# Three expert loads set between the turning transfers of block 10, a pack load ahead of half of block 9's, and the slot sums of block 10 one expert step later

## The chip, the cores and the metric

The kernel runs on one core of a Trainium2 chip. The metric is the device time of one execution in microseconds (us). The kernel before takes 660.15 us, the median of three runs (659.58 to 660.9).

## The reference, cut to what matters

Three layers follow each other on 4608 tokens of width 512, all in float32:

```python
scores = scale * q @ k.T                     # 64 pairs (batch, head), 576 positions, head width 64
x = ((scores * decay) @ v)                   # causal decay gamma_h ** (i - j), then tokens x 512
h = x @ w_in; g = h * sigmoid(1.702 * h)     # 512 -> 2048
x = g @ w_out                                # 2048 -> 512
logits = x @ phi                             # 32 slots
d = softmax over tokens(logits); slot_input = d.T @ x
slot_out[e] = relu(slot_input[e] @ w1[e]) @ w2[e]      # 8 experts, 4 slots each, 512 -> 1024 -> 512
out = softmax over slots(logits) @ slot_out
```

The logits and the softmax over tokens need every token before any expert can start. So the experts' weights (w1 and w2, 64 pieces of 512 KB) and w_out (8 pieces) are used only after the last token.

## The kernel before

The tokens go through in 12 blocks of 384 (`n` = 0 to 11; block 10 is the second last, 11 the last). A block has 16 expert steps `fc`, one for each 128 of the 2048 hidden columns. In each, TensorE (PE) makes 12 products into `hp` (L349), ScalarE (ACT) puts the gated result into `gT` (L359), and VectorE (DVE) turns it into `pre` (L378). Beside this run the steps of the attention of the next block: three steps of 128 tokens to a block, `step_of(g)`, each of which ends by loading the `pack` (q, k and v, 1 MB) of step g + 2 on SyncE's queue (SP, L179). There are two pack buffers; the load of step 35, the last, waits for the products of step 33.

What one half block has in `pre` (8 hidden steps) goes to `nat` in 16 transfers of 96 KB from on-chip memory to on-chip memory, four for each of four row groups `a` (`shuffle`, L386): rows of 1 KB, 32 partitions to 32 others. When both halves lie in `nat`, the slot sums of that block are made one block later: `slots_part(n - 1)`, 12 matmuls into `Sg` (L453, two profile rows to a matmul in float32), and DVE adds them to `acc` (L459). `nat` is one buffer for all blocks. In block 11 the turning is done by PE itself (`turn_fc`, `tpg`, L373) and ACT or DVE copies each result to `nat` (L374), so these copies come after the slot sums of block 10. `Sg`, `tpg` and the attention's results share the same three PSUM buffers.

All order is written out by hand, engine by engine. All transfers and loads stand in one queue, that of SP, and are issued in the order of the code. `prefetch` takes the next piece of a fixed list (8 of w_out, 32 of w1, 32 of w2, three of w1 first) and loads it to the next place that has come free: the buffers of x of block 10 (three pieces), of `pre` (three), of the weights `w` of each expert step of block 11, of `gT`, and so on (L501). After the slot sums of block 11 (`Sg`, L605, in `tail`) come five new places, the reused ones, the expert layers (`h_ps` L666, `so_ps` L707), and the results `op` (L728) with the output transfers (L737).

Of the kernel before, what the change touches and what calls it, by code (L numbers as in the profile page):

```python
# [9 lines left out]
F32 = mybir.dt.float32  # L10
# [22 lines left out]
LAST = NBLK - 1  # L33
NFC = DFF // 128
NDC = DM // 128
NTILE = NT // 128
GF = 4
# [32 lines left out]
EARLY_WINDOWS, EARLY_LOGITS, EARLY_EXP_AT, EARLY_TURN_AT = (2, 6, 10), (((1, 3),), ((0, 0),), ((0, 1),)), 3, 5  # L70
LATE_TURNS = {**{fc: () for fc in range(4)}, 4: (0, 1), 5: (2, 3), 6: (4, 5), 7: (6, 7)}
LAST_LOGITS = {0: ((1, 2), (1, 3)), 4: ((0, 0),), 8: ((0, 1),), 12: ((0, 2),)}
LAST_TURNS = {6: (0, 1), 7: (2, 3), 8: (4, 5), 9: (6, 7), 10: (8,), 11: (9,)}
LAST_EXP_AT, LAST_TURN_AT, LAST_SLOTS_AT = 1, 3, 6
LAST_ACT = (0, 2, 4, 6, 8, 11, 12, 13, 15)
NPRE = NTILE - 2 * NT128

# [52 lines left out]
def tile_kernel(ctx, tc, qkv, w_in, w_turned, w_out, phi, w1, w2, consts, out):  # L130
# [11 lines left out]
    pb = ctx.enter_context(tc.tile_pool(name="pb", bufs=1, side="right", reuse_waits="tile"))  # L142
# [50 lines left out]
    def products(g, parts=("out", "state", "score")):  # L193

        n, cb = g + 1, g % NPB
        own, out_ = [], []
        if "out" in parts and g >= 0:
            t = packs[g]
            Op = Ops[g] = ps.tile([128, NP, NSEQ, C], F32, tag="r", name="Op", bufs=3)
            for p, j in pairs:  # L200
                if cb:
                    out_.append((Op, t, SS, QT, p, j, True))
                out_.append((Op, t, VN, SC, p, j, cb == 0))
        if "state" in parts and g >= 0 and cb < NPB - 1:
            if cb == 0:
                St[g // NPB] = ps.tile([128, NP, NSEQ, D], F32, tag="St", name="St")
            own += [(St[g // NPB], packs[g], KN, VN, p, j, cb + p + j == 0) for p, j in pairs]
        if "score" in parts and n < NSTEP:
            Sp = Sps[n] = ps.tile([128, NP, NSEQ, C], F32, tag="r", name="Sp", bufs=3)
            own += [(Sp, packs[n], KT, QT, p, j, True) for p, j in pairs]  # L210
        for i in range(max(len(own), len(out_))):
            for what, turn in ((own, 0), (out_, 1)):
                if i < len(what):
                    o, w, a, b, p, j, first_ = what[i]
                    for h, oh in ((lo, (lo, hi)[turn]), (hi, (hi, lo)[turn])):
                        pe.matmul(o[oh, p, j, :], w[h, a, p, j], w[h, b, p, j], start=first_, stop=True,  # L216
                                  skip_group_check=True)
# [6 lines left out]
    def scale_scores(n):  # L224
        if n < NSTEP:
            dve.tensor_tensor(packs[n][:, SC], Sps.pop(n), across(dtab), op=ALU.mult)  # L226
# [22 lines left out]
    def step_of(g, between):  # L249
        products(g)  # L250
        scale_keys(g + 1)
        scale_scores(g + 1)
        scale_state(g + 1)
        between()
        scale_out(g)
        x_high(g)
        x_low(g)
        if g + 2 < NSTEP:
            load_step(g + 2)
# [121 lines left out]
    def shuffle(n, hf, rows=range(4)):  # L381
        if n not in nat:
            nat[n] = pm.tile([128, NT128, 4, NFC, 32], F32, tag="nat", name="nat")
        for a in rows:
            for b in range(4):
                sp.dma_start(nat[n][32 * b:32 * b + 32, :, a, hf * HF:(hf + 1) * HF, :],  # L386
                             pre[n, hf][32 * a:32 * a + 32, :, b])
# [60 lines left out]
    def slots_part(n):  # L448
        Sg = ps.tile([128, 4, 4, 32], F32, tag="r", name="Sg", bufs=3)
        for c in range(NT128):  # L450
            nv = nat[n][:, c].rearrange("p a f i -> p f a i")
            for b in range(4):
                pe.matmul(Sg[32 * b:32 * b + 32], dn[n][:, c, :], nv[:, 4 * b:4 * b + 4],  # L453
                          start=(c == 0), stop=(c == NT128 - 1))
        sg = Sg.rearrange("p f a i -> p (f a i)")
        if n == 0:
            dve.tensor_copy(acc, sg)
        else:
            dve.scalar_tensor_tensor(acc, acc, st["corr"], sg, op0=ALU.mult, op1=ALU.add)  # L459
# [19 lines left out]
    wx, places = {}, []  # L479
# [4 lines left out]
    def prefetch(place=None):  # L484
        if not todo:
            return
        key = todo.pop(0)
        if place is None:
            place = places.pop(0)
        t = place()  # L490
        if key not in kept:
            places.append(place)
        if key[0] == 0:
            src = wo_dram[key[1]] if wide else wo_dram[key[1] * 256:(key[1] + 1) * 256, :].rearrange(
                "(c p) d -> p c d", p=128)
        elif key[0] == 1:
            src = w1[key[1], key[2] * 128:(key[2] + 1) * 128, :].rearrange("(c p) d -> p c d", p=128)
        else:
            src = w2[key[1], key[2]]
        t = t.rearrange("p (c d) -> p c d", c=src.shape[1])  # L500
        sp.dma_start(t, src)  # L501
        wx[key] = t

    def prefetch_views(t):
        for i in range(t.shape[1]):
            prefetch(lambda i=i: t[:, i])
# [251 lines left out]
    with tc.manual_schedule(engines={getattr(mybir.EngineType, e) for e in ("PE", "Activation", "DVE", "Pool", "SP")}):  # L758
        for x in START:
            step(x)  # L760
        for n in range(2, LAST):
            early = n == LAST - 1
            windows, logits = (EARLY_WINDOWS, EARLY_LOGITS) if early else (WINDOWS, WINDOW_LOGITS)
            for fc in range(NFC):
                main_fc(n, fc)
                for f in LATE_TURNS.get(fc, (fc,)) if n == 2 else (fc,):
                    turn_fc(n, f)
                if fc in KEEP_AT and n < 2 + NFC // 2 and wide:
                    keep_w_out(2 * (n - 2) + KEEP_AT[fc][0], KEEP_AT[fc][1])
                if fc in windows:  # L770
                    i = windows.index(fc)

                    def between():
                        for m, k in logits[i]:
                            logits_group(n - m, k)
                        if i == 0:
                            softmax_split(n - 1)

                    step_of((n + 1) * STEPS + i, between)
                    if i == 1:  # L780
                        slots_part(n - 1)
                if fc == max(windows[1], HF - 1):
                    shuffle(n, 0)
                if fc == (EARLY_EXP_AT if early else EXP_AT):
                    softmax_exp(n - 1)
                if fc == (EARLY_TURN_AT if early else TURN_AT):
                    softmax_turn(n - 1)
                if fc == NFC - 1:
                    shuffle(n, 1)
                if n == 3 and fc == 0:  # L790
                    prefetch_views(ring4[:, 1:4])
                if n == LAST - 1:
                    if fc == 2:
                        prefetch_views(ring4[:, 0:1])
                        prefetch(place_in(px, "raw", 1))
                    if fc == windows[-1]:
                        att_ctx.close()
                        pw2 = ctx.enter_context(tc.tile_pool(name="pw2", bufs=NW2, side="right", reuse_waits="tile"))
                        for _ in range(NW2):
                            prefetch(place_in(pw2, "w", NW2))  # L800
                        prefetch_views(pb.tile([128, 3, 1024], F32, tag="pre", name="wx", bufs=2))
        n = LAST
        for fc in range(NFC):
            main_fc(n, fc)
            if fc in LAST_LOGITS:
                for m, g in LAST_LOGITS[fc]:
                    logits_group(n - m, g)
            if fc == 0:
                softmax_split(n - 1)
                prefetch_views(pb.tile([128, 3, 1024], F32, tag="x", name="wx", bufs=1))  # L810
            if fc == LAST_EXP_AT:
                softmax_exp(n - 1)
                combine_part(0, NPRE)
            if fc == LAST_TURN_AT:
                softmax_turn(n - 1)
            if fc == LAST_SLOTS_AT:
                slots_part(n - 1)
                prefetch_views(pb.tile([128, 3, 1024], F32, tag="pre", name="wx", bufs=2))
            for f in LAST_TURNS.get(fc, ()):
                turn_fc(n, f)  # L820
            if fc < NFC - 1:
                prefetch(place_in(pw, "w", NFC))
            if fc == GF:
                third = gate().rearrange("p l t -> p (l t)")
                prefetch(lambda: third[:, 0:1024])
        tail()
# [43 lines left out]
```

## Time and profile before

| | |
|---|---|
| median of three runs | 660.15 us (659.58 to 660.9) |
| the profiled execution | 662.24 us, of which 660.5 us span |
| PE busy | 635.4 us (96%) |
| DVE, ACT, POOL busy | 45%, 33%, 12% |
| granted TensorE clock | 0.997 over the span |
| DMA queue of SP | 149.43 MB, 71.1% of 16 engines' span |

PE counts as busy while modelled matmuls run, so 96% leaves little, but not nothing: idle times of PE and stretches in which a group of matmuls takes longer than the same group elsewhere both count. The DMA share is an average: in slices of 16.5 us the page shows 143 to 182 GB/s in the middle of the run and 373 to 411 GB/s in the last eight slices but one.

### The profile page before, as it was taken

What the parts mean: (1) busy time and instruction counts of PE and PEld (TensorE: products, weight loads), DVE (VectorE), ACT (ScalarE), POOL (GpSimd) and SP (SyncE); (2) the same over time, 40 slices, a digit from 0 to 9 for tenths busy, and PEclk for the clock granted to TensorE, in tenths of its full rate; (3) what the DMA queues carried; (4) which work ended last, traced back from release to release, by engine and by line L of the source; (5) the groups of instructions that cost most, each with busy time, mean ns of one, the idle gap of its engine ahead of it and who ended that gap; (6) DMA issues with size and microseconds to landing.
All of it is one profiled execution on the core that took longest, in us unless ns stands there. A gap on an engine that the chain in (4) does not pass through costs nothing.

```text
span 660.5 us, 19533 instructions
## 1 busy us (share of the span) xinstructions
PE 635.4 (96%) x8601; PEld 545.2 (83%) x8601; DVE 295.3 (45%) x592; ACT 221.1 (33%) x430; POOL 80.4 (12%) x72
## 2 busy tenths in 40 slices
PE   6898999999999999999999999999999999999994
PEld 6797787898988989989989989889899788874663
DVE  3899923354463453443444533634535323122143
ACT  2783532141242242332412412412424124240143
POOL 2103101202111011121111011111211000001000
PEclk9999999999999999999999999999999999999998
DMA  8997648676676747737646657467566498999998
GB/s 322 401 314 272 257 97 224 161 197 161 189 243 175 204 164 192 201 113 200 177 135 184 178 143 208 134 163 198 182 175 143 158 287 236 411 406 373 408 410 329
DMA packets 67732, 150.67 MB, mean 228 GB/s; under 512 B 8768, under 2 KB 42944, under 8 KB 63040
## 3 DMA queue, kind: packets, MB, share of 16 engines
q1 hardware_dynamic: 67648, 149.43, 71.1%
q8 instruction: 67, 1.10, 0.7%
q14 instruction: 17, 0.14, 0.1%
HBM read 101.16 MB, written 13.63 MB: 174 GB/s over the span
## 4 chain that ended last, share of the span: by engine, by line
PE 81%; DMA 7%; SPq 4%; DVE 3%; ACT 2%; issue 1%; POOL 0%; DVEq 0%; ACTq 0%
PE hp L349 51%; PE Lg L393 5%; PE Sg L453 4%; SPq L386 4%; PE Sp L216 4%; PE St L216 3%; PE so_ps L707 2%; DMA early_raw<-in_w_turned_dram 2%; PE Op L216 2%; PE h_ps L666 2%; PE op L728 2%; DMA pack<-in_qkv_dram 2%; DMA early_raw<-in_moe_w_in_dram 1%; PE tpg L373 1%; DMA raw<-in_w_turned_dram 1%
## 5 line engine op out<-in xcount | busy, mean ns | idle before, releaser
L349 PE MATMUL hp<-x,w 128*128 128x384 f32 x2304 | 421.3, 340 | 1.3 <-POOL x L246 1.3
L349 PEld LDWEIGHTS hp<-x,w 128*128 128x128 f32 x2304 | 397.1, 188 | 28.6 <-issue 21.7
L378 DVE STREAM_TRANSPOSE pre<-gT 128x384 f32<-128x384 f32 x172 | 96.3, 571 | 166.4 <-ACT gT L359 158.1
L359 ACT ACTIVATE gT<-hp 128x384 f32<-128x384 f32 x188 | 91.8, 491 | 230.6 <-PE hp L349 230.4
L246 POOL TENSOR_TENSOR x<-xs,x 128x512 fp32r<-128x512 f32 x33 | 42.6, 1292 | 317.0 <-ACT x L241 317.0
L216 PE MATMUL Op<-pack 64*64 64x64 f32 x2176 | 72.5, 221 | 0.2 <-issue 0.2
L216 PEld LDWEIGHTS Op<-pack 64*64 64x64 f32 x2176 | 67.2, 136 | 0.6 <-issue 0.6
L222 POOL TENSOR_TENSOR pack<-pack,cs 128x512 f32<-128x512 f32 x32 | 34.7, 1086 | 137.8 <-DMA pack<-in_qkv_dram 128.6
L241 ACT CAST x<-xs 128x512 fp32r<-128x512 f32 x36 | 22.3, 620 | 83.9 <-DVE xs L234 83.8
L216 PE MATMUL Sp<-pack 64*64 64x64 f32 x1152 | 41.4, 223 | 7.3 <-DMA pack<-in_qkv_dram 7.3
L216 PEld LDWEIGHTS Sp<-pack 64*64 64x64 f32 x1152 | 38.0, 139 | 8.6 <-DMA pack<-in_qkv_dram 7.0
L216 PEld LDWEIGHTS St<-pack 64*64 64x64 f32 x1024 | 33.1, 137 | 7.6 <-issue 7.5
L226 DVE TENSOR_TENSOR pack<-Sp,cs 128x512 f32<-128x512 f32 x36 | 24.8, 688 | 32.1 <-PE Op L216 19.1
L393 PE MATMUL Lg<-gT,Wp 128*32 128x384 f32 x376 | 38.5, 495 | 0.4 <-DVE Lall L440 0.4
L216 PE MATMUL St<-pack 64*64 64x64 f32 x1024 | 37.5, 224 | 0.0
L453 PE MATMUL Sg<-nat,dn 128*32 128x512 f32 x264 | 31.2, 593 | 0.0
L234 DVE TENSOR_TENSOR xs<-Op,cs 128x512 f32<-128x512 f32 x36 | 24.6, 682 | 5.6 <-PE Op L216 5.5
L290 ACT ACTIVATE early_raw<-early_raw 128x512 f32<-128x512 f32 x28 | 19.0, 691 | 14.8 <-DMA early_raw<-in_w_turned_dram 9.7
L230 DVE TENSOR_TENSOR pack<-St,cs 128x512 f32<-128x512 f32 x32 | 21.8, 681 | 4.6 <-PE St L216 3.2
L453 PEld LDWEIGHTS Sg<-nat,dn 128*32 128x32 f32 x264 | 8.8, 110 | 17.5 <-issue 17.4
L290 ACT ACTIVATE raw<-raw 128x512 f32<-128x512 f32 x20 | 13.7, 686 | 19.6 <-DMA raw<-in_moe_w_out_dram 18.4
L459 DVE SCALAR_TENSOR_TENSOR acc<-acc,corr,Sg 128x512 f32<-128x512 f32 x10 | 7.5, 748 | 27.6 <-PE Sg L453 27.6
(131 smaller groups left out, 385.6 us busy)
## 6 DMA issues: line engine op xcount, KB each, us to landing
pack<-in_qkv_dram SPq DMA_DIRECT2D x36, 1024.0 KB, 5.9
nat<-pre SPq DMA_DIRECT2D x352, 96.0 KB, 2.2
wx<-in_moe_w_dram SPq DMA_DIRECT2D x56, 512.0 KB, 9.8
raw<-in_moe_w_out_dram SPq DMA_DIRECT2D x16, 512.0 KB, 4.2
early_raw<-in_moe_w_in_dram SPq DMA_DIRECT2D x15, 512.0 KB, 6.8
out_dram<-wx SPq DMA_DIRECT2D x14, 512.0 KB, 7.6
early_raw<-in_w_turned_dram SPq DMA_DIRECT2D x13, 512.0 KB, 9.3
wo_dram<-ring SPq DMA_DIRECT2D x16, 256.0 KB, 2.0
```

What stands on the lines that cost most here:

```text
L216: pe.matmul(o[oh, p, j, :], w[h, a, p, j], w[h, b, p, j], start=first_, stop=True, skip_group_check=True)
L222: pool.tensor_tensor(k, k, by_state(ksc[:, n % NPB, :]), op=ALU.mult)
L226: dve.tensor_tensor(packs[n][:, SC], Sps.pop(n), across(dtab), op=ALU.mult)
L234: dve.tensor_tensor(xss[g], Ops.pop(g), across(osc), op=ALU.mult)
L246: (eng or pool).tensor_tensor(xl[b_][:, :, cols_], xss.pop(g).rearrange("p a j c -> p a (j c)"), xh[b_][:, :, cols_], op=ALU.subtract)
L290: act.activation(upper, upper, AF.Prelu, scale=2.0 ** -112, alpha=2.0 ** 32)
L349: pe.matmul(hp, wt[fc][:, a, dc, :], b[n][:, dc, :], start=(i == 0), stop=(i == 3 * NDC - 1))
L359: act.activation(gT[n, g][:, fl, :], hps.pop((n, fc)), AF.Gelu_apprx_sigmoid)
L378: dve.transpose(pre[n, hf][:, :, :, fh, :].rearrange("p c b i -> p (c b) i"), gT[n, g][:, fl, :].rearrange("p (x j) -> p x j", j=32))
L386: sp.dma_start(nat[n][32 * b:32 * b + 32, :, a, hf * HF:(hf + 1) * HF, :], pre[n, hf][32 * a:32 * a + 32, :, b])
L393: pe.matmul(Lg[n][32 * fl:32 * fl + 32, :], Wp[:, g * GF + fl, :], gT[n, g][:, fl, :], start=(g == 0), stop=(g == NFC // GF - 1))
L453: pe.matmul(Sg[32 * b:32 * b + 32], dn[n][:, c, :], nv[:, 4 * b:4 * b + 4], start=(c == 0), stop=(c == NT128 - 1))
```

## The change

Four edits. First, in block 9 only two of the four row groups of the second half's transfers are issued at the block's end; the other two follow in block 10 behind its first attention step, and so behind the pack load that this step issues. Second, at the end of block 10 the three loads into the buffer of x stand between the four row groups of that block's transfers, one behind each of the first three; before, they stood behind all of them, in block 11. Third, the slot sums of block 10 are made behind expert step 7 of block 11, not 6, and the turning of hidden steps 0 to 3 of block 11 with them. Fourth, the three loads into the buffer of `pre` are issued at expert step 4 instead of 6.

```diff
--- before.py
+++ after.py
@@ -70,8 +70,8 @@
 EARLY_WINDOWS, EARLY_LOGITS, EARLY_EXP_AT, EARLY_TURN_AT = (2, 6, 10), (((1, 3),), ((0, 0),), ((0, 1),)), 3, 5
 LATE_TURNS = {**{fc: () for fc in range(4)}, 4: (0, 1), 5: (2, 3), 6: (4, 5), 7: (6, 7)}
 LAST_LOGITS = {0: ((1, 2), (1, 3)), 4: ((0, 0),), 8: ((0, 1),), 12: ((0, 2),)}
-LAST_TURNS = {6: (0, 1), 7: (2, 3), 8: (4, 5), 9: (6, 7), 10: (8,), 11: (9,)}
-LAST_EXP_AT, LAST_TURN_AT, LAST_SLOTS_AT = 1, 3, 6
+LAST_TURNS = {7: (0, 1, 2, 3), 8: (4, 5), 9: (6, 7), 10: (8,), 11: (9,)}
+LAST_EXP_AT, LAST_TURN_AT, LAST_SLOTS_AT = 1, 3, 7
 LAST_ACT = (0, 2, 4, 6, 8, 11, 12, 13, 15)
 NPRE = NTILE - 2 * NT128
 
@@ -777,6 +777,8 @@
                             softmax_split(n - 1)
 
                     step_of((n + 1) * STEPS + i, between)
+                    if early and i == 0:
+                        shuffle(n - 1, 1, (2, 3))
                     if i == 1:
                         slots_part(n - 1)
                 if fc == max(windows[1], HF - 1):
@@ -785,8 +787,14 @@
                     softmax_exp(n - 1)
                 if fc == (EARLY_TURN_AT if early else TURN_AT):
                     softmax_turn(n - 1)
-                if fc == NFC - 1:
-                    shuffle(n, 1)
+                if fc == NFC - 1 and not early:
+                    shuffle(n, 1, (0, 1) if n == LAST - 2 else range(4))
+                if fc == NFC - 1 and early:
+                    xv = pb.tile([128, 3, 1024], F32, tag="x", name="wx", bufs=1)
+                    for a in range(4):
+                        shuffle(n, 1, [a])
+                        if a < 3:
+                            prefetch(lambda a=a: xv[:, a])
                 if n == 3 and fc == 0:
                     prefetch_views(ring4[:, 1:4])
                 if n == LAST - 1:
@@ -807,7 +815,6 @@
                     logits_group(n - m, g)
             if fc == 0:
                 softmax_split(n - 1)
-                prefetch_views(pb.tile([128, 3, 1024], F32, tag="x", name="wx", bufs=1))
             if fc == LAST_EXP_AT:
                 softmax_exp(n - 1)
                 combine_part(0, NPRE)
@@ -815,6 +822,7 @@
                 softmax_turn(n - 1)
             if fc == LAST_SLOTS_AT:
                 slots_part(n - 1)
+            if fc == GF:
                 prefetch_views(pb.tile([128, 3, 1024], F32, tag="pre", name="wx", bufs=2))
             for f in LAST_TURNS.get(fc, ()):
                 turn_fc(n, f)
```

On SP's queue, in blocks 9 and 10 (nat<-pre are the transfers, pack the attention's load, ring and wx the first two pieces of w_out):

```order
 L179 DMA pack_93<-in_qkv_dram 128x2048
 L333 DMA wo_dram<-ring 128x512
-L386 DMA nat<-pre 32x3x256 x16
+L386 DMA nat<-pre 32x3x256 x8
 L179 DMA pack_92<-in_qkv_dram 128x2048
+L386 DMA nat<-pre 32x3x256 x8
 L501 DMA ring<-wo_dram 128x1024
 L501 DMA wx<-wo_dram 128x1024
```

The last pack load has moved ahead of eight of the sixteen transfers; nothing else of this piece has moved.

On SP's queue at the end of block 10 and in block 11 (wx and gT are places of expert weights):

```order
 L501 DMA wx<-in_moe_w_dram 128x1024 x5
-L386 DMA nat<-pre 32x3x256 x16
+L386 DMA nat<-pre 32x3x256 x4
+L501 DMA wx<-in_moe_w_dram 128x1024
+L386 DMA nat<-pre 32x3x256 x4
+L501 DMA wx<-in_moe_w_dram 128x1024
+L386 DMA nat<-pre 32x3x256 x4
+L501 DMA wx<-in_moe_w_dram 128x1024
+L386 DMA nat<-pre 32x3x256 x4
 L501 DMA wx<-in_moe_w_dram 128x1024 x8
 L501 DMA gT<-in_moe_w_dram 128x1024
-L501 DMA wx<-in_moe_w_dram 128x1024 x17
```

Three loads have moved ahead of the last twelve, eight and four transfers; the 17 loads behind the first gT become 14.

On PE in block 11, from expert step 5 on (hp are the products of an expert step, 12 matmuls; Sg the slot sums of block 10; tpg the turning, three matmuls to a hidden step):

```order
 L393 MATMUL Lg<-gT,Wp 32x384 x4
-L349 MATMUL hp<-x,w 128x384 x24
+L349 MATMUL hp<-x,w 128x384 x36
 L453 MATMUL Sg<-nat,dn 32x512 x12
-L373 MATMUL tpg<-ident,gT 128x128 x6
-L349 MATMUL hp<-x,w 128x384 x12
-L373 MATMUL tpg<-ident,gT 128x128 x6
+L373 MATMUL tpg<-ident,gT 128x128 x12
 L349 MATMUL hp<-x,w 128x384 x12
```

The products of step 7 now stand ahead of the slot sums, and four turnings follow these in a row.

## Rows read from the trace of the kernel before

**Rows 1.** Timeline of PE, 495 to 600: start, length, line, group [idle before <-releaser].
```profile
502.14 0.23 PE L216 MATMUL Op<-pack 64*64 64x64 f32 x2
...
513.29 0.23 PE L216 MATMUL Op<-pack 64*64 64x64 f32 x2
514.66 0.27 PE L216 MATMUL Sp<-pack 64*64 64x64 f32 x2 [1.14 <-DMA pack<-in_qkv_dram]
...
516.42 2.76 PE L453 MATMUL Sg<-nat,dn 128*32 128x512 f32 x24
...
559.46 3.58 PE L453 MATMUL Sg<-nat,dn 128*32 128x512 f32 x24
```

**Rows 2.** Chain of waits in order of time: start, length, engine, line, count.
```profile
502.48 0.62 SPq L386
503.14 1.67 SPq L386
509.47 5.14 DMA pack<-in_qkv_dram
...
516.60 2.57 PE Sg L453 x24
...
555.17 4.36 PE hp L349 x24
559.53 3.51 PE Sg L453 x24
563.04 0.81 PE tpg L373 x6
563.85 2.09 PE hp L349 x12
565.94 0.66 PE tpg L373 x6
```

**Rows 3.** Timeline of SP's queue, 495 to 600 and 588 to 602: start, length, issues.
```profile
496.44 12.93 SPq L386 DMA_DIRECT2D nat<-pre  x16
...
522.66 10.30 SPq L386 DMA_DIRECT2D nat<-pre  x16
...
542.32 16.25 SPq L386 DMA_DIRECT2D nat<-pre  x16
558.68 1.50 SPq L501 DMA_DIRECT2D wx<-in_moe_w_dram  x3
...
596.17 2.63 SPq L501 DMA_DIRECT2D wx<-in_moe_w_dram  x5
```

**Rows 4.** Line 453, 555 to 565: waits before the slot sums, first and last.
```profile
L453 PEldq EVENT_SEMAPHORE  x8: 51/51/51, 556.3 to 560.2; - x8
```

**Rows 5.** Timeline of SP's queue, 558 to 560: the last transfer's issue.
```profile
557.97 0.60 SPq L386 DMA_DIRECT2D nat<-pre  x1
```

**Rows 6.** The page, section 6: DMA issues, KB each, median us from issue to landing.
```profile
nat<-pre SPq DMA_DIRECT2D x352, 96.0 KB, 2.2
```

**Rows 7.** Stretches: length, busy by engine, clock, DMA share, GB/s.
```profile
545.00:550.00 5.00, 5.00 (x30) 5.00 (x29) 1.81 (x6) 3.26 (x7) 0.00 (x0) 1.00 1.02 398
550.00:555.00 5.00, 4.56 (x32) 3.70 (x30) 3.90 (x8) 3.12 (x5) 0.00 (x0) 1.00 0.82 180
555.00:560.00 5.00, 5.00 (x32) 4.25 (x28) 0.00 (x0) 0.93 (x2) 0.00 (x0) 1.00 0.63 126
565.00:570.00 5.00, 5.00 (x38) 4.09 (x37) 0.56 (x1) 1.38 (x4) 0.00 (x0) 1.00 1.03 415
596.00:597.00 1.00, 0.40 (x6) 0.20 (x2) 0.86 (x2) 0.00 (x0) 0.00 (x0) 1.00 0.47 188
650.00:655.00 5.00, 2.45 (x26) 2.12 (x21) 2.49 (x8) 2.09 (x7) 0.00 (x0) 1.00 1.01 405
```

**Rows 8.** Waits of SP's queue, 542 to 560 and 560 to 597: total us, times, longest.
```profile
SPq L386 <- DMA wx<-in_moe_w_dram: 4.2, 5, 1.5
...
SPq L501 <- PE Sg L605: 3.0, 1, 3.0
```

**Rows 9.** Tile nat, 540 to 565: its transfers' time to landing.
```profile
DMA to landing us min/median/max: 2.2/4.0/7.2
```

**Rows 10.** Timeline of DVE and ACT, 555 to 568: what empties PSUM behind the slot sums.
```profile
563.08 0.75 DVE L459 SCALAR_TENSOR_TENSOR acc<-acc,corr,Sg 128x512 f32<-128x512 f32 x1 [8.91 <-PE Sg L453]
563.88 0.56 DVE L374 COPY nat<-tpg 128x384 f32<-128x384 f32 x1
...
563.56 0.48 ACT L374 COPY nat<-tpg 128x384 f32<-128x384 f32 x1 [3.50 <-PE tpg L373]
```

## The prediction

> **What bounds the kernel now.** I read the timeline of PE first, since PE is busy for nearly the whole span, and looked for places where it stands still or where a group takes longer than the same group elsewhere. Between 500 and 597 us there are two that a transfer causes. At 513.5 the scores of attention step 35 stand still 1.14 us for the last pack load [rows 1]. At 559.46 the slot sums of block 10 begin at once, yet the 24 rows of this group take 3.58 us where the same group took 2.76 at 516.42 [rows 1]; in the chain of waits, which does not count overlap twice, it is 3.51 against 2.57 [rows 2]. The 0.94 us between them is a wait inside the group: the semaphores ahead of these matmuls are waited for until 560.2 [rows 4], and the last of the 16 transfers was issued at 557.97 [rows 5], which with the usual 2.2 us to landing [rows 6] gives 560.2 too. So the group starts on the half of `nat` that is there and waits for the other.
>
> Next I read SP's queue, which issues both kinds. The pack load at 509.47 stands behind 16 transfers that took 12.93 us to issue; the last transfers of block 10 took 16.25 us, and the 16 of the first half before them 10.30 [rows 2, 3]. They took so long because they were issued behind loads: the queue waited five times, 4.2 us in all, for loads to land [rows 8].
>
> Last I read the stretches for the DMA engines. They move 398 GB/s to 550 and 415 GB/s from 565 on, but 180 and 126 GB/s from 550 to 560, at busy shares of 0.82 and 0.63 [rows 7]. Then they are full up to 655, but for one hole: in 596 to 597 they move 188 GB/s [rows 7], because the five loads issued at 596.17 waited 3.0 us for the slot sums of block 11 on PE [rows 3, 8]. That hole decides how much the loads are worth. What lies ahead of it, the DMA engines finish in time; what lies behind it starts when PE gets there. Behind it stand 28 loads and the whole output, and these are full-rate work. So the end follows the time at which PE finishes the slot sums of block 11, and PE between 500 and 596 sets that.
>
> **The change part by part.** The sum is made in the profiled execution's time, 662.24 us (span 660.5), and carried over as a difference to the median of 660.15.
>
> Pack load ahead of eight transfers. It removes the wait of 1.14 us. The eighth transfer was issued at 502.48 and the ninth at 503.14 [rows 2]; the pack load now takes that ninth place, where the products of step 33, which free its buffer, are over (502.37, [rows 1]). The issue at 503.14 was a slow one of 1.67 us [rows 2]; if the pack's is as slow it is out by 504.8, and with the 5.14 us that the load took [rows 2] it lands by 510, 3.5 us ahead of the need at 513.5. Gain: 1.14 us. It adds 0.5 us of issue and 2.5 us of traffic (1 MB at 415 GB/s, [rows 7]) ahead of the other eight transfers. These were all issued by 509.4; now by about 510, landing at 512 to 513. The slot sums of block 9 need them at 516.42 − 1.14 = 515.3 [rows 1]. Cost taken: 0. The far end is 1.2 us: if the last of them, issued at 509.3, takes the longest landing that this kind shows behind loads, 7.2 us [rows 9], it lands at 516.5.
>
> Three loads between the transfers. Before, the last transfer landed at 560.2. Two limits say when it does now. By issue: three more issues of 0.5 us each (1.50 for three, [rows 3]) give 557.97 + 1.5 + 2.2 = 561.7. By traffic: a load takes 1.26 us at 415 GB/s, three 3.8 us; in 550 to 560 the DMA engines were free for 5 × 0.18 + 5 × 0.37 = 2.75 us [rows 7], so 1.05 us is left over, and the last lands at about 561.3. I take 561.7. If the loads fill no gap at all, it is 560.2 + 3.8 = 564.0. If they cost nothing, 560.2.
>
> The Trainium skill has a rule that speaks for the far end: by "DMA: Bandwidth & Descriptors", section "Queues, rings and completion order", each DMA engine takes its descriptors in ring order, so a transfer behind a load has to wait for that load. The trace agrees where loads came first: the transfers of block 10 waited for loads five times. By that alone the last transfer would land at 564.0; the gaps between the transfers are why I don't take it.
>
> Slot sums behind step 7. PE reaches them 2.09 us later in its work [rows 2], and all of this stands 1.14 us earlier, since block 10's chain follows PE from 515 on (the first half's transfers at 522.66, the loads behind them, then the second half's). In the old time scale the waiting matmuls are now due at 559.46 + 2.09 + 0.2 = 561.75, the 0.2 being the first two of the group's rows. Against 561.7 nothing is left of the wait; I take 0.1 us, with 2.25 us (564.0) as the far end and 0 as the near one. Gain: 0.94 − 0.1 = 0.84 us.
>
> Four turnings in a row. Before, two pairs took 0.81 and 0.66 us with the products of step 7 between them [rows 2]. Now the third wants the PSUM buffer of the slot sums, which DVE's addition holds from 563.08 to 563.83 [rows 10], 0.8 us after the sums end at 563.04; PE is then through two turnings in 0.66 to 0.81. The fourth wants the buffer of the first, which ACT copied from 563.56 to 564.04 [rows 10]. With some 0.1 us of signal on each this costs 0.25 us; 0 and 0.6 are the bounds. It was covered by step 7's products before; that cover is gone.
>
> Loads of `pre` at step 4, and the three loads themselves. The number of loads ahead of 596 stays the same and they only start earlier; PE waits for none of them between 560 and 596. Taken at 0. What the DMA engines win there becomes a longer hole ahead of the slot sums of block 11.
>
> Sum: −1.14 − 0.84 + 0.25 = −1.73 us, so 660.51 in the profiled execution and 660.15 − 1.73 = 658.4 as the median. Bounds by term: the pack −1.14 to +0.06, the slot sums −0.94 to +1.31, the turnings 0 to 0.6.
>
> **The rivals.** A: the load costs its issue and its transfer one after the other, three times 0.5 + 1.26 = 5.3 us, so the last transfer lands at 565.5. For it: the 16 issues took 16.25 us in place of 10.30 while loads were in front [rows 3]. Against: 0.37 of the engines' time was free from 555 on. The wait is then 3.75 us: −1.14 − 0.94 + 0.25 + 3.75 = +1.9, so 662.1. It turns the change to a loss from a landing at 563.6, and to one that can be measured from 564.9.
>
> B: the transfers land late by the loads' whole 3.8 us, by ring order alone. The wait is 2.25 us: +0.4, so 660.6; with a third of it hidden, 659.3. This is the case of the Trainium skill's rule above.
>
> C: the pack's wait is not there in an ordinary run. For it: it rests on a few slow issues, 12.93 us for 16 where another 16 took 10.30 [rows 3]; without these 2.6 us the load would have been in time. Against: slow issues are in the stretch of block 10 too. The rest is −0.84 + 0.25 = −0.6: 659.55.
>
> D: the DMA engines bound the whole end from 560 on, so that 3.8 us of loads ahead are 3.8 us off the end: 656.3. For it: 405 to 415 GB/s up to 655 [rows 7]. Against: the hole at 596, which shows that they had nothing to do.
>
> **How the numbers follow.** Forecast 0.50, A 0.08, B 0.17, C 0.17, D 0.08. The forecast's own range is −2.1 to −0.9. A measurement of this kernel can tell 0.2%, 1.3 us, from no change. About three quarters of the forecast (0.38), all of D and a little of B and C (0.04) are faster by that: 0.50. Most of A and a little of the unknown is slower: 0.08. The rest is the same: 0.42. The range that leaves out A's upper half and D's lower goes from 656.8 to 660.7.
>
> **What would show it.** In the profile after: no idle time at the scores of step 35, with the pack load issued near 503; the slot sums of block 10 in 2.6 to 2.8 us behind step 7; some 0.25 us of idle PE at the third turning; more than 126 GB/s in the stretch of the transfers; a longer hole ahead of the slot sums of block 11, and those at about 594.5 instead of 596. If the slot sums still take over 4 us, A or B is right. If those of block 11 end as early as said but the end does not move with them, the reading of the hole is wrong.

## The result, and the profile after

The change makes the kernel slower: 664.68 us (median of five, 662.73 to 665.88) against 659.58. The ratio on record is 1.006, with a 95% interval of 1.0039 to 1.0081; the two medians alone stand 0.8% apart. The forecast was 658.4 us.

The timeline of PE in the changed kernel, with the lines that answer to [rows 1, 2] (start, length, group, idle time before it and who ended it):

```profile
513.68 0.85 PE L393 MATMUL Lg<-gT,Wp 128*32 128x384 f32 x8
514.35 2.76 PE L453 MATMUL Sg<-nat,dn 128*32 128x512 f32 x24
...
553.03 6.51 PE L349 MATMUL hp<-x,w 128*128 128x384 f32 x36
559.47 1.05 PE L453 MATMUL Sg<-nat,dn 128*32 128x512 f32 x4
562.94 2.77 PE L453 MATMUL Sg<-nat,dn 128*32 128x512 f32 x20 [2.41 <-DMA nat<-pre]
565.64 1.78 PE L373 MATMUL tpg<-ident,gT 128*128 128x128 f32 x12
...
594.16 2.78 PE L605 MATMUL Sg<-nat,dn 128*32 128x512 f32 x24 [0.35 <-DVE dn L600]
```

The wait for the pack load is gone: the slot sums of block 9 come straight behind the logits. The slot sums of block 10 begin at 559.47 behind step 7, do their first four rows, and then PE waits until 562.94 for a transfer. In this view the group took 3.58 us before and takes 6.24 now (562.94 + 2.77 − 559.47), where it takes 2.78 without a wait. The wait that the step was to cover has grown from 0.8 us (0.94 in the chain of waits) to 3.46.

SP's queue in the same stretch, with the issue of each part (start, length, count):

```profile
501.79 0.33 SPq L179 DMA_DIRECT2D pack<-in_qkv_dram  x1
502.16 5.93 SPq L386 DMA_DIRECT2D nat<-pre  x8
...
540.49 4.41 SPq L386 DMA_DIRECT2D nat<-pre  x4
545.57 0.33 SPq L501 DMA_DIRECT2D wx<-in_moe_w_dram  x1
546.79 4.90 SPq L386 DMA_DIRECT2D nat<-pre  x4
551.73 0.59 SPq L501 DMA_DIRECT2D wx<-in_moe_w_dram  x1
552.37 3.10 SPq L386 DMA_DIRECT2D nat<-pre  x4
555.51 0.96 SPq L501 DMA_DIRECT2D wx<-in_moe_w_dram  x1
556.51 2.56 SPq L386 DMA_DIRECT2D nat<-pre  x4
559.17 5.65 SPq L501 DMA_DIRECT2D wx<-in_moe_w_dram  x8
```

The 16 transfers and three loads are issued from 540.49 to 559.07, 18.6 us where 16.25 were taken before [rows 3]. The last was issued at 558.4. How long they then took, from the same tile and line as [rows 9, 4]:

```profile
DMA to landing us min/median/max: 4.6/6.7/9.6
...
L453 PEldq EVENT_SEMAPHORE  x8: 51/51/3485, 556.3 to 562.8; - x8
```

No transfer lands in less than 4.6 us; before, the median was 4.0 and the quickest 2.2. That alone makes no wait: in d_swap below, which has none, the quickest took 4.1. The stretches of this profile, against [rows 7]:

```profile
550.00:555.00 5.00, 4.57 (x30) 3.65 (x29) 2.02 (x5) 1.08 (x3) 0.00 (x0) 1.00 1.06 257
555.00:560.00 5.00, 5.00 (x31) 4.37 (x29) 0.00 (x0) 1.40 (x3) 0.00 (x0) 1.00 0.99 252
560.00:565.00 5.00, 2.59 (x22) 0.79 (x20) 0.00 (x0) 0.07 (x1) 0.00 (x0) 1.00 1.04 344
580.00:585.00 5.00, 5.00 (x33) 4.12 (x32) 0.00 (x0) 0.98 (x2) 0.00 (x0) 1.00 0.69 250
585.00:590.00 5.00, 5.00 (x34) 4.00 (x33) 1.04 (x2) 2.36 (x4) 0.00 (x0) 1.00 0.77 244
```

The last two of these before:

```profile
580.00:585.00 5.00, 5.00 (x33) 4.38 (x33) 0.00 (x0) 0.98 (x2) 0.00 (x0) 1.00 1.03 410
585.00:590.00 5.00, 5.00 (x32) 3.62 (x31) 1.12 (x2) 3.22 (x6) 0.00 (x0) 1.00 1.01 392
```

From 550 to 560 the DMA engines are now full and move 2.5 MB in place of 1.5. So the loads did go into the free time, but the transfers paid for it. What was won comes back as free time at 580 to 590, where before the engines were full: SP's queue stands there until PE has freed the places for the next loads.

### The profile page after: what moved, and what is told of

Its sections match the earlier page's. It is cut to its first block, busy times and chain, and to the rows that moved or that the text cites. A ratio compares the mean times of both kernels' runs of the same rounds, so it can differ in the third digit from the quotient of the medians.

```text
span 660.9 us, 19536 instructions
## 1 busy us (share of the span) xinstructions
PE 637.6 (96%) x8601; PEld 547.1 (83%) x8601; DVE 295.0 (45%) x592; ACT 221.7 (34%) x430; POOL 80.3 (12%) x72
## 4 chain that ended last, share of the span: by engine, by line
PE 82%; DMA 7%; DVE 4%; SPq 3%; issue 1%; ACT 1%; POOL 0%; ACTq 0%; DVEq 0%
PE hp L349 52%; PE Lg L393 5%; PE Sg L453 4%; PE St L216 4%; PE Sp L216 4%; DMA wx<-in_moe_w_dram 3%; PE so_ps L707 2%; PE op L728 2%; PE h_ps L666 2%; PE Op L216 2%; DMA pack<-in_qkv_dram 2%; SPq L386 2%; PE tpg L373 1%; SPq L501 1%; DVE pre L378 1%
## 5 line engine op out<-in xcount | busy, mean ns | idle before, releaser
L453 PE MATMUL Sg<-nat,dn 128*32 128x512 f32 x264 | 31.4, 593 | 2.4 <-DMA nat<-pre 2.4
L453 PEld LDWEIGHTS Sg<-nat,dn 128*32 128x32 f32 x264 | 8.7, 110 | 20.2 <-issue 16.8
L736 DVE COPY wx<-op 128x256 f32<-128x256 f32 (+1 forms) x32 | 11.3, 402 | 19.7 <-PE op L728 19.1
```

## The experiments

Kernels whose labels begin with the same letter were measured in turn with the kernel before on one chip; c, d, e and f are four chips, so ratios are compared between them and not times. The table gives the ratio to before, and from the timeline of PE in each profile the stretch from the begin of the slot sums of block 9 to the begin of those of block 11, with the length of the slot sums of block 10 in it (begin of the first row to end of the last; 2.8 us is no wait). Both leave out the wait for the pack load, which lies ahead of the stretch. Between kernels with the slot sums behind step 6 and behind step 7 the stretch differs by the four turnings in a row too.

| kernel | loads ahead of the last transfer, against before | ratio (95%) | stretch, us | slot sums 10, us |
|---|---|---|---|---|
| before, profile above | 0 | | 76.86 | 3.58 |
| c_before | 0 | 1.0001 (0.998 to 1.0021) | 77.96 | 4.66 |
| c_pack | 0 | 1.0003 (0.9984 to 1.0022) | 77.20 | 3.91 |
| c_behind | 0 | 0.9984 (0.9966 to 1.0002) | 76.36 | 2.78 |
| d_swap | 0 | 0.9977 (0.9953 to 1.0002) | 76.36 | 2.78 |
| d_one | 1 | 0.9974 (0.9953 to 0.9995) | 76.35 | 2.78 |
| f_one | 1 | 0.997 (0.9955 to 0.9985) | 76.39 | 2.78 |
| e_two | 2 | 1.0019 (0.9993 to 1.0045) | 77.49 | 3.94 |
| d_ahead | 3 | 1.001 (0.9989 to 1.003) | 79.09 | 5.53 |
| changed | 3 | 1.006 (1.0039 to 1.0081) | 79.81 | 6.24 |
| d_after | 3 | 1.0057 (1.0033 to 1.008) | 81.76 | 8.21 |
| f_after | 3 | 1.0067 (1.0045 to 1.0089) | 79.81 | 6.28 |
| e_warm (3.4 us of idle matmuls ahead) | 3 | 1.006 (1.0035 to 1.0086) | 79.87 | 3.10 |
| f_warm (the same kernel as e_warm) | 3 | 1.0065 (1.0038 to 1.0092) | 85.41 | 8.65 |
| c_nopack | 3 | 1.0066 (1.0045 to 1.0087) | 79.15 | 5.62 |
| e_six | −3 | 0.997 (0.9945 to 0.9994) | 76.09 | 2.78 |
| f_six | −3 | 0.9974 (0.9958 to 0.999) | 78.31 | 2.78 |

**c_before**, the kernel before once more, with no edit.

> The kernel before once more, unchanged: a second profile of it, and the span and granted clock of each of its runs. Theory T (the last transfers of block 10 land too late once three loads lie among them): ratio 1.000; a run has no wait of 1.14 us for the pack load, or a smaller one, since the profile shown was 2.6 us above the median; granted clock 0.995 or more in all runs. Rival K (the granted clock falls late in a run, by chance, and costs 1.3 to 3 us): some of these runs, too, show a clock under 0.99 and times 1.3 to 3 us above the others.

Measured: 660.81 us beside 660.51. Its profile has no wait at all for the pack load, and the slot sums of block 10 wait again:

```profile
515.22 2.76 PE L453 MATMUL Sg<-nat,dn 128*32 128x512 f32 x24
...
558.28 1.05 PE L453 MATMUL Sg<-nat,dn 128*32 128x512 f32 x4
560.17 2.77 PE L453 MATMUL Sg<-nat,dn 128*32 128x512 f32 x20 [0.84 <-DMA nat<-pre]
```

So the 1.14 us were no steady cost, while the wait in the slot sums of block 10 is longer here: 1.9 us. The mean clocks go from 0.992 to 0.997 and not from 0.995 as expected, but in the 35 runs beside it the 11 with a mean clock of 0.993 or less have a median of 660.5 us, as the others have, so rival K has nothing here.

**c_pack**, the first edit alone.

```diff
-                    shuffle(n, 1)
+                    shuffle(n, 1, (0, 1) if n == LAST - 2 else range(4))
...
+                    if early and i == 0:
+                        shuffle(n - 1, 1, (2, 3))
```

> The kernel before with the first edit alone: the last pack load ahead of eight of block 9's sixteen transfers. Theory T: the pack load is not what made the change slow, so 0 to 1.1 us faster than before (ratio 0.998 to 1.000), no wait at the scores of step 35. Rival P (the eight transfers behind the pack land late and hold up what follows): 1 us or more slower, with a wait at the slot sums of block 9. Rival K: single runs slower by 1.3 to 3 us at a clock under 0.99, as in any variant.

Measured: 1.0003. The edit neither helps nor harms in a way that can be measured. Its profile has no wait for the pack load and none in the slot sums of block 9, so the sign of rival P is missing.

**c_behind**, the changed kernel with its three loads behind all transfers.

```diff
-                    xv = pb.tile([128, 3, 1024], F32, tag="x", name="wx", bufs=1)
-                    for a in range(4):
-                        shuffle(n, 1, [a])
-                        if a < 3:
-                            prefetch(lambda a=a: xv[:, a])
+                    shuffle(n, 1)
+                    prefetch_views(pb.tile([128, 3, 1024], F32, tag="x", name="wx", bufs=1))
```

> The changed kernel, but with its three loads behind all sixteen transfers of block 10 instead of between them; the slot sums stay behind step 7. Theory T: the slot sums of block 10 don't wait (2.6 to 2.8 us for the group), and the time is 0.5 to 1.7 us under that of before (ratio 0.997 to 0.9995), 4 us or more under the changed kernel. Rival S (it is the later slot sums and the four turnings in a row that cost): still 2 us or more slower than before. Rival K: no better than the changed kernel in the runs with a clock under 0.99.

Measured: 0.9984, 0.76% under the changed kernel's ratio (against the kernel before it is not clear of no change), and no wait:

```profile
513.14 2.76 PE L453 MATMUL Sg<-nat,dn 128*32 128x512 f32 x24
...
558.27 2.78 PE L453 MATMUL Sg<-nat,dn 128*32 128x512 f32 x24
...
589.50 2.78 PE L605 MATMUL Sg<-nat,dn 128*32 128x512 f32 x24 [0.35 <-DVE dn L600]
```

Rival S falls: with the same later slot sums and the same four turnings the loss is gone. What made it is the place of three issues on SP's queue.

**c_nopack**, the changed kernel without its first edit (the lines of c_pack taken back).

> The changed kernel without its first edit: the last pack load behind all sixteen transfers of block 9 again, the three loads between the transfers of block 10, the slot sums behind step 7. Theory T: as slow as the changed kernel or slower by up to 1.1 us, ratio to before 1.004 to 1.009, the slot sums of block 10 in over 5 us. Rival P (the pack ahead is what costs): back within 0.2% of before.

Measured: 1.0066, as slow as the changed kernel. Rival P falls. Its profile has a wait for the pack load again, half as long as in the first profile of the kernel before:

```profile
513.00 0.27 PE L216 MATMUL Sp<-pack 64*64 64x64 f32 x2 [0.59 <-DMA pack<-in_qkv_dram]
```

**d_one**, one load between the transfers (behind the eighth), two behind all.

```diff
-                        if a < 3:
-                            prefetch(lambda a=a: xv[:, a])
+                        for i in {1: [0], 3: [1, 2]}.get(a, []):
+                            prefetch(lambda i=i: xv[:, i])
```

> The changed kernel with one load between the transfers of block 10 (behind the eighth) and two behind all sixteen. Theory Q (each load anywhere ahead of the last transfer puts its landing off by the load's whole 1.26 us): the last transfer lands 1.3 us later than with all loads behind, where it was 0.7 us in time, so a wait of 0.6 us in the slot sums of block 10 and a ratio to before of 0.999 to 1.001. Theory M (it is the mixing that makes the transfers slow, whatever the number): a wait of 2 us or more, ratio 1.003 or more.

Measured: 0.9974 and no wait. One load is hidden whole, better than theory Q had it.

```profile
558.95 2.78 PE L453 MATMUL Sg<-nat,dn 128*32 128x512 f32 x24
```

**d_ahead**, the three loads ahead of all transfers, none between.

```diff
-                    xv = pb.tile([128, 3, 1024], F32, tag="x", name="wx", bufs=1)
-                    for a in range(4):
-                        shuffle(n, 1, [a])
-                        if a < 3:
-                            prefetch(lambda a=a: xv[:, a])
+                    prefetch_views(pb.tile([128, 3, 1024], F32, tag="x", name="wx", bufs=1))
+                    shuffle(n, 1)
```

> The changed kernel with its three loads ahead of all sixteen transfers of block 10, none between. Theory Q: the last transfer still has all three ahead of it, so the slot sums wait 2.9 to 3.5 us as in the changed kernel, ratio 1.005 to 1.008. Theory M: the transfers run unmixed, so a wait under 1.5 us and a ratio of 1.000 to 1.003.

Measured: 1.001, between the two theories. The profile has theory Q's wait, nearly:

```profile
560.00 1.05 PE L453 MATMUL Sg<-nat,dn 128*32 128x512 f32 x4
562.76 2.77 PE L453 MATMUL Sg<-nat,dn 128*32 128x512 f32 x20 [1.72 <-DMA nat<-pre]
```

The group takes 5.5 us, a wait of 2.75, where 2.9 to 3.5 were expected and under 1.5 by theory M. But the ratio is the one that theory M had. On this chip the median is 1.3 us above that of the kernel before, and the changed kernel's (d_after) 4.7 us, with as many loads ahead of the last transfer. So most of the wait comes with the loads' being ahead at all, but the larger part of the lost time comes only when they stand between the transfers.

**d_swap**, three loads between as in the change, but the three into the other `pre` buffer moved from ahead of the transfers to behind them.

```diff
-                        prefetch_views(pb.tile([128, 3, 1024], F32, tag="pre", name="wx", bufs=2))
...
                             prefetch(lambda a=a: xv[:, a])
+                    prefetch_views(pb.tile([128, 3, 1024], F32, tag="pre", name="wx", bufs=2))
```

> The changed kernel with its three loads between the transfers, but the three loads into the other pre buffer, which stood ahead of the transfers, behind them. As many loads are ahead of the last transfer as before the change. Theory Q: no wait in the slot sums of block 10 (2.6 to 2.8 us for the group), ratio 0.997 to 0.9995. Theory M: a wait of 2 us or more, ratio 1.003 to 1.007.

Measured: 0.9977 and no wait, with the three loads between the transfers as in the changed kernel.

```profile
560.48 2.78 PE L453 MATMUL Sg<-nat,dn 128*32 128x512 f32 x24
```

So the mixing by itself costs nothing that can be measured here: whether there is a wait goes by the number of loads ahead of the last transfer. What the wait costs when there are three too many depends on the mixing too, as d_ahead shows.

**d_after**, the changed kernel again.

> The changed kernel once more. A wait of 2.9 to 3.5 us in the slot sums of block 10, ratio 1.004 to 1.008. Theory H (standing still that long also brings TensorE's granted clock to its lower level for some us behind it, in many of the runs): the profile may show 0.5 between 560 and 570 us; runs with a mean clock of 0.99 or less are 2 us or more above those with 0.995.

Measured: 1.0057. This profile, unlike the first, shows what theory H said:

```profile
560.32 1.05 PE L453 MATMUL Sg<-nat,dn 128*32 128x512 f32 x4
564.06 4.47 PE L453 MATMUL Sg<-nat,dn 128*32 128x512 f32 x20 [2.70 <-DMA nat<-pre]
```

```profile
560.00:565.00 5.00, 2.30 (x15) 0.55 (x17) 0.00 (x0) 0.49 (x1) 0.00 (x0) 0.97 1.04 314
565.00:570.00 5.00, 4.96 (x28) 2.03 (x21) 1.30 (x2) 0.52 (x2) 0.00 (x0) 0.69 1.02 412
```

The granted clock is 0.97 and 0.69 in these stretches (third column from the right); read in steps of 1 us it is 0.50, the lower level of 1.2 GHz, from 565 to 568. That is right behind PE's wait: from the first of the group's rows at 560.32 to the fifth at 564.06 are 3.74 us. The 20 rows from there take 4.47 us in place of 2.77: 1.7 us more for the same work, and the stretch is 81.76 in place of 79.81. In the first profile the same wait was 3.47 us and the clock stayed.

The runs go the way of theory H too: the six with a mean clock of 0.99 or less have a median of 666.4 us, the two with 0.995 or more 663.5. With the other runs of the changed kernel, from two more series of runs, it is 666.0 for ten and 663.3 for five. The mean doesn't tell where the clock fell: in the first profile, at 0.990, it was full in all of 550 to 600.

**e_two**, two loads between (behind the fourth and the eighth transfer), the third behind all.

```diff
-                        if a < 3:
-                            prefetch(lambda a=a: xv[:, a])
+                        for i in {0: [0], 1: [1], 3: [2]}.get(a, []):
+                            prefetch(lambda i=i: xv[:, i])
```

> The changed kernel with two loads between the transfers of block 10 (behind the fourth and the eighth) and the third behind all sixteen. If the gaps between the transfers hide some 2.7 us of loads and no more: a wait of 0 to 1 us in the slot sums, ratio 0.998 to 1.000, so that the third load carries most of the price. If each load costs the same beyond a fixed slack: a wait of 1.5 to 2 us, ratio 1.000 to 1.003.

Measured: 1.0019, the slot sums 3.94 us long, a wait of 1.16.

```profile
560.17 3.94 PE L453 MATMUL Sg<-nat,dn 128*32 128x512 f32 x24
```

The wait lies between the two expectations, the ratio in the second's range.

**e_six**, all six loads behind the transfers, and the slot sums behind step 6 again.

```diff
-LAST_TURNS = {7: (0, 1, 2, 3), 8: (4, 5), 9: (6, 7), 10: (8,), 11: (9,)}
-LAST_EXP_AT, LAST_TURN_AT, LAST_SLOTS_AT = 1, 3, 7
+LAST_TURNS = {6: (0, 1), 7: (2, 3), 8: (4, 5), 9: (6, 7), 10: (8,), 11: (9,)}
+LAST_EXP_AT, LAST_TURN_AT, LAST_SLOTS_AT = 1, 3, 6
...
+                    shuffle(n, 1)
+                    prefetch_views(pb.tile([128, 3, 1024], F32, tag="x", name="wx", bufs=1))
+                    prefetch_views(pb.tile([128, 3, 1024], F32, tag="pre", name="wx", bufs=2))
```

> The kernel with the pack load ahead of half of block 9's transfers, and with the three loads of x and the three of the other pre buffer all behind the sixteen transfers of block 10; the slot sums of block 10 behind step 6, as before the change. Theory Q (what is queued ahead of the last transfer decides when it lands): it lands 3.8 us earlier than before, so no wait in the slot sums even there, 2.6 to 2.8 us for the group, and a ratio of 0.996 to 0.999. If the transfers of block 10 are slow of themselves: a wait of 0.8 to 1.9 us as before, ratio 0.999 to 1.001.

Measured: 0.997, no wait even behind step 6. The row of PE, and those of SP's queue:

```profile
559.14 2.78 PE L453 MATMUL Sg<-nat,dn 128*32 128x512 f32 x24
```

```profile
537.04 1.46 SPq L501 DMA_DIRECT2D wx<-in_moe_w_dram  x2
541.95 12.09 SPq L386 DMA_DIRECT2D nat<-pre  x16
554.14 12.18 SPq L501 DMA_DIRECT2D wx<-in_moe_w_dram  x14
```

With three loads fewer in front, the same 16 transfers are out in 12.09 us in place of 16.25 and the last is issued at 553.4. This is theory Q's result from the other side.

**e_warm**, the changed kernel with idle matmuls in PE's wait.

```diff
             if fc == LAST_SLOTS_AT:
+                t = ps.tile([128, NB], F32, tag="h", name="again", bufs=3)
+                for _ in range(5):
+                    pe.matmul(t, ident, Wp.rearrange("p f s -> p (f s)")[:, 0:NB], start=True, stop=True)
                 slots_part(n - 1)
```

> The changed kernel with five idle matmuls of 128x384 (some 3.8 us; their result is not read) on PE ahead of the slot sums of block 10, which fill the wait for the last transfer with work. Theory H (part of the loss is the granted clock that falls behind the wait): no 0.5 between 560 and 570 us in the profile, no runs with a clock of 0.987 to 0.988, and 1.5 to 3 us less than the changed kernel: ratio to before 1.001 to 1.004. Rival N (the wait alone is the loss): as slow as the changed kernel or slower by up to 0.5 us, ratio 1.005 to 1.008.

Measured: 1.006 (1.0035 to 1.0086). The clock kept its upper level there, and no run had a mean clock under 0.99, but the time is the changed kernel's. So theory H, as an explanation of the median, gets nothing from this, though the runs of d_after spoke for it. The two were then run beside each other on one chip, with d_one and e_six again.

> The changed kernel, beside the one with idle matmuls in the wait, on one chip. Theory H (a good part of the loss is the granted clock that falls behind the wait): 1.5 us or more above that one in the median, and several runs with a mean clock of 0.988 or less. Rival N (the wait alone): within 0.7 us of it, whatever the clocks.

> The changed kernel with five idle matmuls on PE ahead of the slot sums of block 10, whose result is not read. Theory H: 1.5 us or more under the changed kernel beside it, no run with a clock of 0.988 or less. Rival N: within 0.7 us of the changed kernel, or above it.

> The changed kernel with one load between the transfers of block 10 and two behind all sixteen. Theory Q (what is queued ahead of the last transfer decides): no wait in the slot sums, ratio to before 0.996 to 0.9995, 5 us or more under the changed kernel. Were the order on the queue not the cause: within 3 us of the changed kernel.

> The three loads of x and the three of the other pre buffer behind all sixteen transfers of block 10, the slot sums behind step 6, the pack load ahead. Theory Q: no wait in the slot sums, ratio to before 0.995 to 0.999; within 0.7 us of the kernel with one load between, since both have no wait and start the slot sums of block 11 at the same time.

Measured: 665.5 us for the changed kernel (six runs, one of them with a mean clock under 0.988), 665.04 with the idle matmuls (seven runs), 658.65 with one load between, 659.5 with six behind. The half us between the first two is rival N's. The last two stand 0.85 us apart, where at most 0.7 was expected. The profile of f_warm shows that the idle matmuls were not always enough (they fill 3.39 us; its run was the slowest of seven):

```profile
560.42 3.39 PE L826 MATMUL again<-Wp,ident 128*128 128x384 f32 x10
563.74 1.05 PE L453 MATMUL Sg<-nat,dn 128*32 128x512 f32 x4
567.92 4.47 PE L453 MATMUL Sg<-nat,dn 128*32 128x512 f32 x20 [3.14 <-DMA nat<-pre]
```

Here the last transfer comes 4.0 us later still, counted from the slot sums of block 9 (567.92 − 515.38, against 562.94 − 514.35), and the clock falls behind that second wait. Transfers and loads stand on the queue as in the changed kernel, but it took 21.0 us to issue the 16 and the three (541.33 to 562.37) in place of 18.6, and then the landing took longer too. So much can it spread between executions.

## Why the prediction was wrong

**What bounds: right.** I said that the end follows the begin of the slot sums of block 11. From there to the end of the span the changed kernel takes 660.9 − 594.16 = 66.7 us, c_behind 656.2 − 589.50 = 66.7, the kernel before 660.5 − 593.28 = 67.2, although the free time of the DMA engines ahead of it differs. The begin before, from its chain of waits:

```profile
593.28 2.83 PE Sg L605 x24
```

In all profiles it is 66.6 to 68.2, while the begin moves by 11 us, from 589.4 in f_one to 600.8 in f_warm. Earlier loads alone are worth nothing: d_one, with one load more ahead of the last transfer, has the same stretch as c_behind to 0.01 us. (The GB/s that the text ahead of the prediction gives from the page's slices are misread: the middle half of the run has 113 to 243, and 373 to 411 are five of the last six slices. No term used them.)

**The pack load: right in the trace, not in the time.** The load was issued at 501.79 and the wait is gone, as in all 14 profiles with this edit. But in the three profiles without it the wait is 1.14, 0 and 0.59 us (before, c_before, c_nopack), so 1.14 was its largest size and not its usual one, and c_pack shows no gain; one of half a us would be too small to see in its 0.2%. Rival C named this: a wait that hangs on slow issues of one execution. The far end of the term came up once too: in the profile of f_six the slot sums of block 9 wait in the middle, and its stretch is 78.31 in place of 76.09 for the same program.

```profile
515.09 1.03 PE L453 MATMUL Sg<-nat,dn 128*32 128x512 f32 x4
517.32 2.77 PE L453 MATMUL Sg<-nat,dn 128*32 128x512 f32 x20 [1.21 <-issue]
```

The eight transfers behind the pack load were issued until 513.5 there, in the other profiles with this edit until 506.6 to 510.8. That PE waited for the last of them fits this; the trace names no releaser, and no run tested it.

**The landing of the last transfer: the step that failed.** "By traffic ... in 550 to 560 the DMA engines were free ... so 1.05 us is left over, and the last lands at about 561.3. I take 561.7." Counted from the begin of the slot sums of block 9, the 16 transfers start where they did before (26.1 us behind it, before 25.9), so that the forecast can be laid beside the run: the last should have landed 45.3 us behind that begin (561.7 − 516.42). It was there after 562.8 − 514.35 = 48.45 us, or 564.9 in the old time scale, later than rival B's 564.0 and short of rival A's 565.5. PE came to the slot sums nearly when it was forecast to, so the wait that I put at 0.1 us was 3.46.

On the same scale, by the last wait for a semaphore at L453: with no load more ahead of it the last transfer is there after 43.8 to 44.9 us (before, c_before, c_pack), with two after 45.6, with three after 47.8 to 48.8 (48.6 in e_warm, 52.4 in f_warm); with one (d_one, f_one), or with three fewer (e_six), it was there before PE needed it. So three loads put it off by some 4 us. That is near their whole 3.8 us, as rival B had it, with something of the issue on top, as rival A had it: 2.3 us of it are longer issuing. It is not an even 1.26 us for each: the first costs PE nothing, the third 2.3 to 3.3 us. What SP's issuing does and what the traffic on the DMA engines does is not told apart, since no run put the loads on another engine's queue.

My reading of the free time, which no run tests by itself: it lay in the pauses between issues, above all near the end of the stretch, and a load set between transfers on one queue pushes every transfer behind it. The trace agrees with the rule that I set against my value, that an engine takes what is queued in order (the Trainium skill, "DMA: Bandwidth & Descriptors", "Queues, rings and completion order"): the delay is about the loads' own time. The five waits that I named for it [rows 8] are waits of SP's queue before it issues, and speak less for it than this delay does. I had both numbers and took the nearer end.

**The slot sums a step later: right in the trace, not shown in the time.** Without the loads in between they have no wait (c_behind), which is what the 0.84 us stood for. But e_six has none behind step 6 either and gains as much, so the gain of 0.16% to 0.3% that c_behind, d_one, f_one and e_six show comes with the wait's going, however that is done, and not with the step.

**The four turnings in a row: right in size.** c_behind and e_six have no wait and differ in the turnings: 76.36 − 76.09 = 0.27 us; I had added 0.25.

**What stays open.** In the first profile of each, the changed kernel's stretch is 79.81 − 76.86 = 2.95 us longer than before: 2.66 of wait and 0.27 of turnings. The medians are 5.1 us apart. On the chip of the last four runs the changed kernel loses 4.45 us to the median before and 6.85 to f_one, but its profile there shows a stretch only 79.81 − 76.39 = 3.4 us longer than f_one's. Two of the three profiles of the changed kernel happen to fall on quick runs (662.73, the lowest of five; 662.44, the lowest of six); the third, on a usual one (666.06 beside a median of 665.9), has the late landing and the half clock and a stretch of 81.76. A later landing still, as in f_warm, and the half clock, as in d_after, both make up such an amount. The runs by their clock speak for the half clock, the idle matmuls against it, and these cost time of their own where the landing is early. How often each happens was not shown.

## What to carry to other kernels

Free time of the DMA engines between small transfers is little room for loads on the same queue, when something waits for the last of the small ones. Here one load was hidden, two cost a wait of 1.2 us and three one of 2.75 to 3.7: count loads ahead of it at their full time, and put them behind. A wait seen in one profile is worth its length only if it is there in a second profile of the same program. And where the work behind a point starts when the engine gets there, data that arrives earlier than that point needs is worth nothing.

## What the runs showed of the hardware that was not expected

Two stretches in which the DMA engines were full, with transfers of 1 KB rows and loads mixed, moved very different amounts: 257 GB/s at a share of 1.06 in 550 to 555 of the changed kernel, 194 GB/s at the same share in the same stretch of f_warm, the run whose last transfer came 4.0 us later. How much of each was transfers and how much loads was not separated. A wait of PE of 3.74 us was followed by the lower clock level in d_after, one of 3.47 us in the first profile was not.
